# Longformer attention and snake MLP on one core: w_out matmuls placed earlier, index arithmetic moved to batch 0, global columns split

## The chip, the core and the metric

The kernel runs on one core of a Trainium2 chip. The metric is device time in microseconds (us) of one execution. The engines are PE (TensorE: matmuls, with their weight loads listed as PEld), DVE (VectorE), ACT (ScalarE), POOL (GpSimd) and SP (SyncE, which here only issues DMAs). Each engine works through its own list in order.

## The reference, cut to what matters

Attention over 8 batches, 8 heads, 576 tokens, head width 64. A query sees the keys within 32 positions, and 8 global tokens see and are seen by all. The result, as 4608 rows of 512, goes through an MLP:

```python
scores = where(|i - j| <= 32 or i is global or j is global, q @ k.T / 8, -1e9)
x = (softmax(scores) @ v).transpose(0, 2, 1, 3).reshape(4608, 512)
h = x @ w_in                                  # 512 -> 2048
g = h + sin(alpha * h) ** 2 / (alpha + 1e-9)
out = g @ w_out                               # 2048 -> 512
```

## The kernel before, in words

The kernel writes the order of every engine's work by hand: what the code says first is first in the engine's list. It goes batch by batch, and each batch has two stages.

**Attention** of a batch (`attention`, for batch 0 `attention_first`) runs over four head pairs `hp`. A pair has two rounds of `scores` (14 small matmuls into one PSUM tile `ring`, then Exp on ACT, L980, and the mask product on DVE, L981), the sums of the numerators and denominators (`products`, L1009, 28 small matmuls each), a logarithm and an exponential on ACT as the reciprocal (L813, L820), and a product on DVE into `xT` (L1027). There is one `ring` tile, so a round's matmuls start only when the Exp before them has been read out. DVE also takes the sums of the global queries (`GN`, `GD`, L797).

**gemm1** of a batch (`gemm1`) makes `h` in 16 groups `nt` of 128 columns of w_in. A group is 8 matmuls (L1161) into one of three PSUM tiles `zn`, `zr`, `zd` in turn; then Sin on ACT (L1194), a square on ACT or DVE (L1197, L1199), and a multiply and add on DVE into `H` (L1200), which frees the PSUM tile for the group three later. In the last batch `xT` has 64 more columns, the global queries of all batches, made by `global_rows` (L1066, L1068).

**gemm2** (`gemm2`) multiplies `H` with w_out, in blocks of 128 rows: 16 matmuls 128x512 each (L1247) into one of two tiles `zo`, then a copy on ACT to `osb` (L1252) and stores. Even batches have 4 blocks, odd ones 5. It is a Python generator: `fill(n)` takes n of its matmuls and puts them where the code stands. So the w_out matmuls of batch b fill the gaps that PE has in the attention of batch b + 1 and in its gemm1. How many go where is written in tables: `START` one ahead of the first scores, `FIRST[hp]` after the first round of scores of a pair, `SECOND[hp]` after the second, `NEAR` and `MIDST` around the last pair, `PER_GROUP[nt]` after each gemm1 group, `GROUP_LAST[nt]` in the last batch. The copy of a block is put down when the 17th matmul is asked for, ahead of it. What a batch doesn't use up is carried on to the next.

**The tail.** After the last gemm1 come, on PE, all w_out matmuls still waiting, then the 32 matmuls of `gemm2_globals` (L1272), then gemm2 of batch 7 (80 matmuls, the last block in two halves) with a few matmuls of `judge` in between. `put_globals` (L1234) has POOL copy 8 columns of `H`, each to a column whose place is read from a register; it needs the last group's `H`, and gemm2 of batch 7 needs it. `square_x` (DVE) and `square_w` (ACT) feed `judge`, a check of ranges.

`load_columns` computes from the global indices those column places: seven DVE operations on 1x8 numbers (L1213 to L1225), then 8 register loads on POOL. It stands in the attention of batch 5 (batches count from 0), before the last pair's work is done. In batch 0, `load_lying` (L713) has POOL issue four DMAs with the keys and queries of batch 1: two when the scores of batch 0 are done, two when its last products are done. They land where PE transposes them in gemm1 of batch 0 (`turn_lying`, L729).

Of the kernel before, what the change touches and what calls it, by code (L numbers as in the profile page):

```python
# [10 lines left out]
ALU = mybir.AluOpType  # L11
# [238 lines left out]
def kernel(  # L250
# [11 lines left out]
    nc = tc.nc  # L262
    B, H, S, D = q.shape
# [6 lines left out]
    NHP = H // 2  # L270
# [35 lines left out]
    SG = S + NG * B  # L306
# [154 lines left out]
    for half in range(2):  # L461
        for w, src in ((1, k), (0, q)):
            nc.gpsimd.dma_start(
                out=nat[w][D * half : D * half + HK],
# [23 lines left out]
    for t in (gidx8, gp64):  # L488
        nc.vector.memset(t[:].bitcast(DT.int32), 0)
    nc.sync.dma_start(  # L490
        out=g64[:],
# [286 lines left out]
    xTs = {}  # L778
# [160 lines left out]
    def attention(b, beside):  # L939
# [117 lines left out]
        inverse(last)  # L1057
        nc.scalar.preload_act_table(AF.Sin)
        fill(MIDST)
        numerators(last)  # L1060
        beside(NHP)
        after.release()

    def global_rows(bs):

        nc.vector.reciprocal(out=GR[:, :, :, bs], in_=GD[:, :, :, bs])  # L1066
        if bs.stop == B:
            nc.vector.tensor_tensor(  # L1068
                out=xTs[B - 1][:, :, S:SG], in0=GN[:].rearrange("p h j b -> p h (j b)"),
                in1=GR[:].rearrange("p h j b -> p h (j b)"), op=ALU.mult,  # L1070
            )


    spare = [kflat, vflat]
# [68 lines left out]
    def gemm1(b):  # L1143


        while len(waiting) > 1:
            fill(1)
        xT = xTs[b]
        r0 = (b % 2) * S
        more = b == B - 1  # L1150
        W = SG if more else S
        hr = tc.alloc_tile_pool(name="hr", bufs=1, space=PSUM)
        hs = {}

        def chunks(nt, cs, parts=slice(0, 2)):
            if nt not in hs:
                hs[nt] = (zn, None, zd)[nt % 3] or hr.tile([P, 2, 512], DT.float32, name="zr")
            h = hs[nt]
            for c in cs:
                for h_part, lo, hi in halves(h, W)[parts]:  # L1160
                    nc.tensor.matmul(  # L1161
                        out=h_part, lhsT=w_in[:, c, nt * P : (nt + 1) * P], rhs=xT[:, c, lo:hi],
                        start=(c == 0), stop=(c == CT - 1), skip_group_check=True,
                    )

        on_act = (ON_ACT_FIRST, ON_ACT_SECOND, ON_ACT)[min(b, 2)]
        for nt in range(NT):
            if b == 1 and nt in (10, 12):
                for which, t, y in PLACES[nt - 6 : nt - 4]:
                    place(2, which, t, y, nc.vector.tensor_copy)  # L1170
            if b == 0 and 8 <= nt < 14:
                third, late = divmod(nt - 8, 2)
                place_lying(1 - late, third, nc.scalar.copy if late else nc.vector.tensor_copy)
            if b == 0 and nt == 4:
                turn_kq()
            if b == 0 and nt == 10:

                cast_globals_v()
                for part in range(3):
                    place_globals(1, part, nc.gpsimd.tensor_copy)  # L1180
                load_vg(1)
            if nt == 0:

                for n in range(2):
                    chunks(n, range(CT - 1), slice(0, 2 - more))
                for n in range(2 * more):
                    chunks(n, range(CT - 1), slice(1, 2))
            chunks(nt, range(CT - 1, CT) if nt < 2 else range(CT))
            h = columns(hs[nt], W)
            fill((GROUP_LAST if more else PER_GROUP)[nt])  # L1190
            if b == 0 and nt in (7, 9, 11):
                turn_lying((nt - 7) // 2)
            sb = spool.tile([P, SG], DT.bfloat16, name="sb")
            nc.scalar.activation(out=sb[:, 0:W], in_=h, func=AF.Sin, scale=alphaT[:, nt : nt + 1])  # L1194
            s2 = spool.tile([P, SG], DT.bfloat16, name="s2")
            if nt in on_act:
                nc.scalar.activation(out=s2[:, 0:W], in_=sb[:, 0:W], func=AF.Square)  # L1197
            else:
                nc.vector.tensor_tensor(out=s2[:, 0:W], in0=sb[:, 0:W], in1=sb[:, 0:W], op=ALU.mult)  # L1199
            nc.vector.scalar_tensor_tensor(  # L1200
                out=H2[:, nt, r0 : r0 + W], in0=s2[:, 0:W], scalar=recipT[:, nt : nt + 1], in1=h,
                op0=ALU.mult, op1=ALU.add,
            )
        hr.release()


    columns_of = []

    def load_columns():

        ci = normp.tile([1, 4, NG], DT.int32, name="ci")
        cf = normp.tile([1, 4, NG], DT.float32, name="cf")
        nc.vector.tensor_copy(out=ci[:, 0], in_=gi32[:, 0::2])  # L1213
        nc.vector.tensor_scalar(out=ci[:, 1], in0=ci[:, 0], scalar1=1, scalar2=None, op0=ALU.bitwise_and)
        nc.vector.tensor_copy(out=cf[:, 0:2], in_=ci[:, 0:2])
        nc.vector.tensor_scalar(
            out=cf[:, 2], in0=cf[:, 0], scalar1=float(HALF), scalar2=float(QTR), op0=ALU.is_ge, op1=ALU.mult
        )
        nc.vector.scalar_tensor_tensor(
            out=cf[:, 3], in0=cf[:, 0], scalar=0.5, in1=cf[:, 2], op0=ALU.mult, op1=ALU.add  # L1220
        )
        nc.vector.scalar_tensor_tensor(
            out=cf[:, 3], in0=cf[:, 1], scalar=float(QTR) - 0.5, in1=cf[:, 3], op0=ALU.mult, op1=ALU.add
        )
        nc.vector.tensor_scalar(out=gcol[:], in0=cf[:, 3], scalar1=float(S), scalar2=None, op0=ALU.add)  # L1225
        for j in range(NG):
            columns_of.append(nc.gpsimd.value_load(gcol[0:1, j : j + 1], min_val=S, max_val=2 * S - 1))

# [7 lines left out]
    def gemm2(b):  # L1236
        lo, hi = (0, 4) if b % 2 == 0 else (4, 9)
        for blk in range(lo, hi):
            ops = zo[(blk + b // 2) % 2]
            osb = osbp.tile([P, DM], DT.float32, name="osb")  # L1240
            parts = 2 if (b, blk) == (B - 1, hi - 1) else 1
            for part in range(parts):
                cols = slice(part * DM // parts, (part + 1) * DM // parts)
                if part:
                    ops = zd[:, 1]
                for nt in range(NT):
                    nc.tensor.matmul(  # L1247
                        out=ops[:, cols], lhsT=H2[:, nt, blk * P : (blk + 1) * P], rhs=w_out[:, nt, cols],
                        start=(nt == 0), stop=(nt == NT - 1), skip_group_check=True,
                    )  # L1250
                    yield True
                nc.scalar.copy(out=osb[:, cols], in_=ops[:, cols])  # L1252
                store(b, blk, osb, cols)

    def store(b, blk, osb, cols):
# [27 lines left out]
        )  # L1283


    waiting = []

    def fill(n):
        while n and waiting:
            if next(waiting[0], None) is None:  # L1290
                waiting.pop(0)
            else:
                n -= 1

    START = 1
    FIRST, SECOND = (10, 6, 4, 4), (4, 4, 4, 4)

    NEAR, MIDST = 3, 6
    PER_GROUP = (0, 0, 5) + 11 * (1,) + (0, 0)
    GROUP_LAST = (0, 0, 3) + 13 * (1,)  # L1300

    def places_at(b_att, at):
# [5 lines left out]
    def phase_a(b_att, b_moe):  # L1308
        def beside(at):

            if b_moe is None:
                if at == 0:
                    second_half()
                    gather(v, gv)
                if at == NHP - 1:
                    load_lying(0)
                if at == NHP:
                    load_lying(1)
                    cast_v(1)
                    for half in range(2):  # L1320
                        rows = slice(half * D, (half + 1) * D)
                        nc.sync.dma_start(out=MASKT[rows], in_=MASK[rows, half * NT6 : (half + 1) * NT6])
                    load_w_out()
                    load_v(1)
                return
            if at == 2 and b_att == B - 1:
                global_rows(slice(0, B - 1))
            if b_att == 5 and at == 3:
                load_columns()
            if 0 <= at < 2:  # L1330
                square_x(b_moe, at)
            if at == 2 and 1 < b_att and b_att + 2 < B:
                pace(xTs[b_att][0:1, 0, 0:1])
                cast_qk(b_att + 2)
                cast_v(b_att + 2)
            if b_moe == 0 and at == 1:
                turn_qk(2)
            for which, t, y in places_at(b_att, at):
                place(b_att + 1, which, t, y, nc.vector.tensor_copy)

        if b_moe is not None:
            waiting.append(gemm2(b_moe))
        attention(b_att, beside)

    phase_a(0, None)
    for b in range(B):
# [5 lines left out]
        if 0 < b < B - 1:  # L1352
            load_v(b + 1)
            load_vg(b + 1)
        if b == B - 1:
            global_rows(slice(b, B))
        gemm1(b)
        if b + 1 < B:
            if b == 0:
# [54 lines left out]
```

## Time and profile before

| | us |
|---|---|
| median of 3 runs | 361.01 (360.44 to 361.14) |
| the profiled execution, its own time | 360.89 |
| its span, from first to last instruction | 359.1 |
| PE busy in the span | 325.6 |
| ACT busy | 286.4 |
| DVE busy | 274.8 |
| POOL busy | 58.9 |

The profiled execution's own time is 1.8 us above its span, and 0.12 us below the median. A PE that is busy is not a PE at its peak, since ends of matmuls are modelled: in the timeline's rows a matmul's end lies after the start of the next. A delay on PE is therefore best read from starts.

### The profile page before, as it was taken

What the parts mean: (1) busy time and instruction counts of PE and PEld (TensorE: products, weight loads), DVE (VectorE), ACT (ScalarE), POOL (GpSimd) and SP (SyncE); (2) the same over time, 40 slices, a digit from 0 to 9 for tenths busy, and PEclk for the clock granted to TensorE, in tenths of its full rate; (3) what the DMA queues carried; (4) which work ended last, traced back from release to release, by engine and by line L of the source; (5) the groups of instructions that cost most, each with busy time, mean ns of one, the idle gap of its engine ahead of it and who ended that gap; (6) DMA issues with size and microseconds to landing.
All of it is one profiled execution on the core that took longest, in us unless ns stands there. A gap on an engine that the chain in (4) does not pass through costs nothing.

```text
span 359.1 us, 10959 instructions
## 1 busy us (share of the span) xinstructions
PE 325.6 (91%) x4484; PEld 206.8 (58%) x4484; DVE 274.8 (77%) x536; ACT 286.4 (80%) x428; POOL 58.9 (16%) x85
## 2 busy tenths in 40 slices
PE   2668888999899999999999999899999998999992
PEld 1557655556555765577557655576567655664552
DVE  6876866887979787978798788878887876788620
ACT  7779768987889898988998889688988887887510
POOL 7965410051004000400040004000000000004200
PEclk9999989999999999999999999999999999999998
DMA  7999999669988936695759754993251021002132
GB/s 111 114 142 158 160 222 239 143 107 206 189 147 163 171 71 153 126 187 100 133 112 185 146 103 90 197 144 84 63 112 42 2 62 35 29 0 58 51 87 67
DMA packets 87764, 42.27 MB, mean 118 GB/s; under 512 B 72378, under 2 KB 82362, under 8 KB 87322
## 3 DMA queue, kind: packets, MB, share of 16 engines
q0 software_dynamic: 44944, 18.52, 43.1%
q1 hardware_dynamic: 42762, 22.98, 29.1%
q8 instruction: 37, 0.61, 0.7%
q14 instruction: 21, 0.17, 0.2%
HBM read 41.97 MB, written 20.77 MB: 175 GB/s over the span
## 4 chain that ended last, share of the span: by engine, by line
PE 57%; ACT 14%; DVE 13%; DMA 7%; issue 5%; POOL 2%; DVEq 0%; ACTq 0%; POOLq 0%
PE zo L1247 25%; PE zn L1161 9%; DVE H L1200 6%; PE zr L1161 6%; PE zd L1161 5%; ACT sb L1194 5%; PE ring L971 3%; DMA VD<-in_q_dram 3%; DMA H<-in_q_dram 3%; PE zd L1009 2%; DVE s L1199 2%; ACT L947 2%; ACT E L980 2%; ACT s L1197 2%; PE zn L1009 2%
## 5 line engine op out<-in xcount | busy, mean ns | idle before, releaser
L1247 PE MATMUL zo<-w_out,H 128*128 128x512 bf16 (+1 forms) x576 | 148.8, 377 | 0.2 <-DVE E L981 0.2
L1161 PEld LDWEIGHTS <-w_in 128*128 128x128 bf16 x1024 | 99.5, 98 | 49.2 <-issue 16.4
L1247 PEld LDWEIGHTS <-H 128*128 128x128 bf16 x592 | 52.5, 98 | 44.9 <-issue 0.5
L1161 PE MATMUL zn<-xT,w_in 128*128 128x288 bf16 (+1 forms) x384 | 57.0, 287 | 6.9 <-DVE H L1200 3.6
L1194 ACT ACTIVATE sb<-zn,alphaT 128x576 bf16<-128x576 f32 (+1 forms) x48 | 35.7, 743 | 19.5 <-PE zn L1161 19.3
L1161 PE MATMUL zr<-xT,w_in 128*128 128x288 bf16 x320 | 47.8, 288 | 2.1 <-DVE H L1200 2.1
L980 ACT ACTIVATE E<-ring 128x720 bf16<-128x720 f32 x56 | 43.4, 775 | 7.4 <-PE ring L971 6.6
L1200 DVE SCALAR_TENSOR_TENSOR H<-s,recipT,zn 128x576 bf16<-128x576 bf16 (+1 forms) x48 | 39.5, 822 | 11.6 <-ACT s L1197 8.2
L1161 PE MATMUL zd<-xT,w_in 128*128 128x288 bf16 x320 | 47.2, 292 | 0.4 <-DVE H L1200 0.3
L1197 ACT ACTIVATE s<-sb 128x576 bf16<-128x576 bf16 (+1 forms) x58 | 40.0, 689 | 1.8
L981 DVE TENSOR_TENSOR E<-E,MASKT 128x720 bf16<-128x720 bf16 x56 | 29.6, 529 | 14.4 <-ACT E L980 14.1
L1199 DVE TENSOR_TENSOR s<-sb 128x576 bf16<-128x576 bf16 (+1 forms) x70 | 32.0, 458 | 10.5 <-ACT sb L1194 10.5
L1200 DVE SCALAR_TENSOR_TENSOR H<-s,recipT,zr 128x576 bf16<-128x576 bf16 (+1 forms) x40 | 32.9, 822 | 8.8 <-ACT s L1197 6.8
L1200 DVE SCALAR_TENSOR_TENSOR H<-s,recipT,zd 128x576 bf16<-128x576 bf16 (+1 forms) x40 | 32.9, 822 | 6.1 <-ACT s L1197 3.7
L1194 ACT ACTIVATE sb<-zr,alphaT 128x576 bf16<-128x576 f32 (+1 forms) x40 | 29.6, 741 | 8.1 <-PE zr L1161 8.1
L1194 ACT ACTIVATE sb<-zd,alphaT 128x576 bf16<-128x576 f32 (+1 forms) x40 | 29.5, 738 | 4.6 <-PE zd L1161 4.6
L1252 ACT COPY osb<-zo 128x512 f32<-128x512 f32 (+1 forms) x36 | 20.7, 576 | 13.0 <-PE zo L1247 6.7
L820 ACT ACTIVATE R<-L,shift 128x576 f32<-128x576 f32 x32 | 24.9, 778 | 0.5
L347 POOL COPY seen<-xT 1x1 bf16<-1x1 bf16 x4 | 1.7, 428 | 126.6 <-DVE GN L797 126.6
L1234 POOL COPY H<-H 128x16 bf16 x8 | 5.0, 630 | 103.8 <-DVE H L1200 103.4
L1027 DVE TENSOR_TENSOR xT<-zn,R 128x576 bf16<-128x576 f32 x21 | 15.8, 753 | 0.8 <-ACT R L820 0.6
L343 POOL DMA_DIRECT2D vd<-in_v_dram x7 | 16.4, 2337 | 0.1
(185 smaller groups left out, 373.0 us busy)
## 6 DMA issues: line engine op xcount, KB each, us to landing
vd<-in_v_dram POOLq DMA_DIRECT2D x7, 576.0 KB, 14.0
kd<-in_k_dram POOLq DMA_DIRECT2D x6, 576.0 KB, 7.3
qd<-in_q_dram POOLq DMA_DIRECT2D x6, 576.0 KB, 10.2
VX<-vd SPq DMA_DIRECT2D x16, 168.0 KB
w_in<-in_moe_w_in_dram POOLq DMA_DIRECT2D x4, 512.0 KB, 6.7
w_out<-in_moe_w_out_dram POOLq DMA_DIRECT2D x4, 512.0 KB, 19.0
VD<-vd SPq DMA_DIRECT2D x12, 168.0 KB
out_dram<-osb SPq DMA_DIRECT2D x7, 256.0 KB
```

The source lines that it names most:

```text
L343: nc.gpsimd.dma_start(out=cast[b, "vd"][:], in_=v[b].rearrange("h s d -> s h d"))
L820: nc.scalar.activation(out=R[:], in_=L[:], func=AF.Exp, scale=-1.0, bias=shift[:, 0:1])
L980: nc.scalar.activation(out=Eg, in_=zs[:, :, 0 : G3 * WCOL], func=AF.Exp, scale=scale)
L981: nc.vector.tensor_tensor(out=Eg, in0=Eg, in1=MASKT[:, None, G3 * g : G3 * (g + 1), :].rearrange("p o m c -> p o (m c)").to_broadcast([P, ...
L1027: nc.vector.tensor_tensor(out=xT[:, hp, 0:S].rearrange("p (k m c) -> p k m c", k=4, c=KT), in0=tokens(nd(hp, 0)), in1=Rs[hp][:], op=ALU.mult,)
L1161: nc.tensor.matmul(out=h_part, lhsT=w_in[:, c, nt * P : (nt + 1) * P], rhs=xT[:, c, lo:hi], start=(c == 0), stop=(c == CT - 1), skip_group ...
L1194: nc.scalar.activation(out=sb[:, 0:W], in_=h, func=AF.Sin, scale=alphaT[:, nt : nt + 1])
L1197: nc.scalar.activation(out=s2[:, 0:W], in_=sb[:, 0:W], func=AF.Square)
L1199: nc.vector.tensor_tensor(out=s2[:, 0:W], in0=sb[:, 0:W], in1=sb[:, 0:W], op=ALU.mult)
L1200: nc.vector.scalar_tensor_tensor(out=H2[:, nt, r0 : r0 + W], in0=s2[:, 0:W], scalar=recipT[:, nt : nt + 1], in1=h, op0=ALU.mult, op1=ALU.add,)
L1247: nc.tensor.matmul(out=ops[:, cols], lhsT=H2[:, nt, blk * P : (blk + 1) * P], rhs=w_out[:, nt, cols], start=(nt == 0), stop=(nt == NT - 1) ...
L1252: nc.scalar.copy(out=osb[:, cols], in_=ops[:, cols])
```

## The change

Five edits, each a place in an engine's list:

1. `FIRST[0]` goes from 10 to 12: two more w_out matmuls ahead of the second scores of the first pair, in batches 1 to 7.
2. `AFTER_COPY`: in gemm1, two groups after one in which a block's copy was put down, two more w_out matmuls.
3. `PER_GROUP` puts one more at group 14.
4. The seven DVE operations on the column places become `find_columns` and move into the attention of batch 0, at the end of the third pair; the register loads stay.
5. In the last batch the reciprocal of the global sums and the products of three of the four pairs' global columns go ahead of the last numerators; the fourth pair's product follows them. Before, one reciprocal and one product came after all.

```diff
         fill(MIDST)
+        if b == B - 1:
+            global_rows(slice(b, B))
+            global_columns(slice(0, last))
         numerators(last)
+        if b == B - 1:
+            global_columns(slice(last, NHP))
         beside(NHP)
...
     def global_rows(bs):
         nc.vector.reciprocal(out=GR[:, :, :, bs], in_=GD[:, :, :, bs])
-        if bs.stop == B:
-            nc.vector.tensor_tensor(
-                out=xTs[B - 1][:, :, S:SG], in0=GN[:].rearrange("p h j b -> p h (j b)"),
-                in1=GR[:].rearrange("p h j b -> p h (j b)"), op=ALU.mult,
-            )
+
+    def global_columns(hps):
+        nc.vector.tensor_tensor(
+            out=xTs[B - 1][:, hps, S:SG], in0=GN[:, hps].rearrange("p h j b -> p h (j b)"),
+            in1=GR[:, hps].rearrange("p h j b -> p h (j b)"), op=ALU.mult,
+        )
...
         for nt in range(NT):
+            at_group[0] = (b, nt)
...
             fill((GROUP_LAST if more else PER_GROUP)[nt])
+            if nt and copied[0] == (b, nt - 2):
+                fill(AFTER_COPY)
...
-    def load_columns():
+    def find_columns():
...
+    def load_columns():
         for j in range(NG):
...
                 nc.scalar.copy(out=osb[:, cols], in_=ops[:, cols])
+                copied[0] = at_group[0]
...
-    FIRST, SECOND = (10, 6, 4, 4), (4, 4, 4, 4)
+    FIRST, SECOND = (12, 6, 4, 4), (4, 4, 4, 4)
+    AFTER_COPY = 2
...
-    PER_GROUP = (0, 0, 5) + 11 * (1,) + (0, 0)
+    PER_GROUP = (0, 0, 5) + 12 * (1,) + (0,)
...
                 if at == 0:
                     second_half()
                     gather(v, gv)
+                if at == 2:
+                    find_columns()
...
-        if b == B - 1:
-            global_rows(slice(b, B))
         gemm1(b)
```

What this makes of the lists, at three places. Names are tiles; `[waits X]` says on which engine's semaphore an instruction waits.

**PE, the tail.** Before, from the last of the waiting w_out matmuls (L1247, 37 of them after the last gemm1 group) through the 32 of `gemm2_globals` (L1272) to the first of batch 7's gemm2:

```order
L1247 LDWEIGHTS H_97
L1247 MATMUL zo_124<-w_out,H_97 128x512
L1272 LDWEIGHTS H_97
L1272 MATMUL zd<-w_out,H_97 64x256 [waits DVE_49]
...
L1247 LDWEIGHTS H_97 [waits Pool_49]
L1247 MATMUL zo_125<-w_out,H_97 128x512 [waits Activation_49]
```

With the change, from the last gemm1 group (L1168) on; what stands in the rows left out first is five more w_out matmuls (L1261), then `gemm2_globals` (L1287):

```order
L1168 LDWEIGHTS w_in
L1168 MATMUL zn<-xT,w_in 128x352
L1261 LDWEIGHTS H_97
L1261 MATMUL zo_124<-w_out,H_97 128x512
...
L1287 LDWEIGHTS H_97
L1287 MATMUL zd<-w_out,H_97 64x256 [waits DVE_49]
...
L1261 LDWEIGHTS H_97 [waits Pool_49]
L1261 MATMUL zo_125<-w_out,H_97 128x512 [waits Activation_49]
```

Between the last group and `gemm2_globals` 6 w_out matmuls are left of 37: 31 stand earlier, 14 of them in the attention of batches 1 to 7 (two each), and in gemm1 of batches 1 to 7 there are -2, +3, +3, +3, +3, +5 and +2. The weight load that waits for POOL stands where it stood.

**DVE, the end of the attention of batch 7.** Before, with the last numerators' product (`xT<-zd`) and the global columns (`xT<-GN,GR`):

```order
L797 TENSOR_REDUCE GD<-zr 128x2x4
L1027 TENSOR_TENSOR xT<-zd,R 128x576
L797 TENSOR_REDUCE GN<-zd 128x2x4
L1066 RECIPROCAL GR<-GD 128x32
L1068 TENSOR_TENSOR xT<-GN,GR 128x4x64
```

With the change:

```order
L797 TENSOR_REDUCE GD<-zr 128x2x4
L1071 RECIPROCAL GR<-GD 128x32
L1075 TENSOR_TENSOR xT<-GN,GR 128x3x64
L1027 TENSOR_TENSOR xT<-zd,R 128x576
L797 TENSOR_REDUCE GN<-zd 128x2x4
L1075 TENSOR_TENSOR xT<-GN,GR 128x64
```

Only the last 64 columns' product is left behind the last numerators.

**DVE, batch 0**, between the second pair's product into `xT` (L897) and the three mask products (L847) of the fourth pair:

```order
 L897 TENSOR_TENSOR xT<-zn,R 128x576
+L1224 COPY ci<-girow 1x8
+L1225 TENSOR_SCALAR ci<-ci 1x8
+L1226 CAST cf<-ci 1x16
+L1227 TENSOR_SCALAR cf<-cf 1x8
+L1230 SCALAR_TENSOR_TENSOR cf<-cf 1x8
+L1233 SCALAR_TENSOR_TENSOR cf<-cf 1x8
+L1236 TENSOR_SCALAR gcol<-cf 1x8
 L847 TENSOR_TENSOR E<-E,MASK 128x480 x3
```

The seven rows are those that stood in the attention of batch 5, ahead of its last two products into `xT`.

More of the change, by code (lines that the diff above doesn't have):

```diff
@@ L1204, in gemm1 @@
         hr.release()
+        at_group[0] = None
     columns_of = []
-    def load_columns():
+    def find_columns():
         ci = normp.tile([1, 4, NG], DT.int32, name="ci")
@@ L1283, in gemm2_globals @@
         )
-    waiting = []
+    waiting, copied, at_group = [], [None], [None]
     def fill(n):
```

## The prediction

> **What bounds the kernel now.** I read the page first, then the chain of waits, then the timeline at the places that the change touches.
>
> ```profile
> span 359.1 us, 10959 instructions
> PE 325.6 (91%) x4484; PEld 206.8 (58%) x4484; DVE 274.8 (77%) x536; ACT 286.4 (80%) x428; POOL 58.9 (16%) x85
> PE 57%; ACT 14%; DVE 13%; DMA 7%; issue 5%; POOL 2%; DVEq 0%; ACTq 0%; POOLq 0%
> ```
>
> PE is busy for 91% of the span and holds 57% of the chain: from batch 1 on it is the bound, broken by short waits. The change adds no PE work, so it can win only waits of PE. The second thing to read is the end, in the chain of waits.
>
> ```profile
> 324.73 7.99 PE zo L1247 x37
> 332.72 1.87 PE zd L1272 x32
> 334.58 7.01 PE zo L1247 x32
> ...
> 352.87 0.37 ACT osb L1252
> ```
>
> After the last gemm1 group, at T = 324.73, PE has no gap to 352.85: 37 w_out matmuls at 7.99/37 = 0.216 us each, the 32 of the globals, then batch 7's gemm2 from 334.58 on, 9.85 after T. A w_out matmul taken from these 37 seems to be worth 0.216 us. But behind them another chain is hidden, seen in the timeline:
>
> ```profile
> 326.53 0.88 DVE L1200 SCALAR_TENSOR_TENSOR H<-s,recipT,zn 128x640 bf16<-128x640 bf16 x1
> 327.48 5.46 POOL L1234 COPY H<-H 128x16 bf16 x8 [103.39 <-DVE H L1200]
> ```
>
> POOL's eight copies start when the last H is made and end at 332.94, T + 8.21. Batch 7's gemm2 waits for them. PE comes to it 1.6 us later now, so the wait costs nothing. This is the point on which the forecast turns.
>
> **The change, part by part.** T moves by the PE work that is put ahead of it, less the waits that go.
>
> *Work ahead of T.* 31 matmuls (37 - 6) x 0.216 = +6.70.
>
> *Second scores (edit 1).* In a batch's first pair PE waits for ACT:
>
> ```profile
> 98.35 2.33 PE L1247 MATMUL zo<-w_out,H 128*128 128x512 bf16 x10
> 100.01 0.77 ACT L980 ACTIVATE E<-ring 128x720 bf16<-128x720 f32 x1
> 100.83 0.35 PE L971 MATMUL ring<-QX,KD 64*64 64x120 bf16 x14
> ...
> 287.82 0.35 PE L971 MATMUL ring<-QX,KX 64*64 64x120 bf16 x14
> ```
>
> The ten matmuls take 2.16 from 98.35, to 100.51; elsewhere scores start 0.09 after a w_out matmul is through, so 0.22 of the start at 100.83 is the wait for the Exp that ends at 100.78. The same 0.22 stands in batches 2, 3, 5, 6 and 7 (the last row is batch 7's), 0.15 in batch 4 and none in batch 1: 5 x 0.22 + 0.15 = -1.25. Two matmuls (0.43) cover it, so each batch's attention gets about 0.2 longer.
>
> *Copies and group 14 (edits 2 and 3).* A block's copy on ACT holds up a Sin, and so a PSUM tile:
>
> ```profile
> 131.46 0.57 ACT L1252 COPY osb<-zo 128x512 f32<-128x512 f32 x1
> 134.13 1.14 PE L1161 MATMUL zn<-xT,w_in 128*128 128x288 bf16 x8 [0.48 <-DVE H L1200]
> ...
> 312.48 0.38 PE L1247 MATMUL zo<-w_out,H 128*128 128x512 bf16 x1
> 313.06 1.25 PE L1161 MATMUL zr<-xT,w_in 128*128 128x288 bf16 x8 [0.21 <-DVE H L1200]
> ```
>
> The first copy, at 131.46, is followed by the wait at 134.13. At 313.06 a group starts 0.58 after a matmul of 0.216: 0.37 of waiting. From the first (0.64) to this there are nine such waits, at the third group after a copy or at group 15: 0.64 in batch 2, 0.40 in 3, 0.43 and 0.26 in 4, 0.39 and 0.22 in 5, 0.43 and 0.25 in 6, 0.37 in 7, together 3.39. Two matmuls stand now where 0.37 to 0.43 was waited, one where 0.22 to 0.26 was: -3.39. What is late next is PE itself. In batch 1, where two fewer stand, DVE's placing copies set the pace at the end, and I count no wait won or lost.
>
> *Column places (edit 4).* In batch 5 seven small operations stand between other work of DVE:
>
> ```profile
> 224.03 0.15 DVE L1213 COPY ci<-girow 1x8 int32<-1x8 int32 x1
> 225.37 0.46 DVE L369 COPY KD<-kt 64x1152 bf16<-64x1152 bf16 x1
> 227.74 0.53 PE L1161 MATMUL zn<-xT,w_in 128*128 128x288 bf16 x3 [1.17 <-DVE GN L797]
> ```
>
> The seven hold DVE 225.37 - 224.03 = 1.34 us, and gemm1 then waits 1.17 for the product and sum behind them. Without them that is 1.34 earlier, the numerators on PE are next, and 1.13 goes. POOL's register loads stay, and POOL stands idle for 103.39 between them and the copies that use them (row above).
>
> In batch 0 the same 1.34 lands here (rows of the timeline, of the chain, and of the DMA issues with KB and us to landing):
>
> ```profile
> 29.35 1.22 DVE L847 TENSOR_TENSOR E<-E,MASK 128x480 bf16<-128x480 bf16 x3
> 30.20 0.79 PE L878 MATMUL zr<-E,OB 128*128 128x88 bf16 x14
> 31.38 0.63 ACT L813 ACTIVATE L<-zr 128x576 f32<-128x576 f32 x1
> 32.08 0.58 POOL VD L713
> 32.66 10.86 DMA VD<-in_q_dram
> 43.02 0.21 PE L729 MATMUL zo<-identb,KD 48*64 48x48 bf16 x1
> 43.56 0.21 PE L729 MATMUL zo<-identb,VD 48*64 48x48 bf16 x1 [0.34 <-DMA VD<-in_q_dram]
> KD<-in_k_dram POOLq DMA_DIRECT2D x1, 288.0 KB, 9.7
> VD<-in_q_dram POOLq DMA_DIRECT2D x1, 288.0 KB, 10.9
> ```
>
> The masks would end at 31.91 instead of 30.57. PE, ready for these products at 30.20, is through 1.2 later, and so is POOL's issue of the last two loads at 32.08; behind them on POOL's queue stand batch 1's values and w_out. ACT's logarithm of these sums, at 31.38, can start at 32.27, 0.9 later, and with it gemm1. PE's transposes, reached at 43.02, wait until 43.56 for the load that lands at 43.52. Between nothing and the whole 1.2 I take +0.45, near the row of that wait: PE comes 0.9 late, and 0.5 of waiting covers half of it. The landing itself should hardly move: the first load was issued 2.5 ahead of the last and needed 9.7, the last 10.9, so they drain one behind another, and the last has to queue anyway.
>
> *Global columns (edit 5).* The chain of waits shows what gemm1 of batch 7 waits for:
>
> ```profile
> 302.10 0.76 DVE xT L1027
> 302.86 0.13 DVE GN L797
> 302.99 0.27 DVE GR L1066
> 303.29 0.43 DVE xT L1068
> ...
> 303.77 0.61 PE zn L1161 x3
> ```
>
> The six half groups ahead are through by 302.63. With the reciprocal and three pairs' product ahead of 302.10, in DVE's wait for the numerators, PE goes on; the last quarter's product is due about 303.25, ahead of the matmul that needs it. 303.77 - 302.63 = -1.14.
>
> So T moves by 6.70 - 1.25 - 3.39 - 1.13 - 1.14 + 0.45 = **+0.24**. The waits removed are just paid for by the work moved ahead.
>
> *The tail.* After T there are 6 x 0.216 + 1.87 = 3.2 us of PE work, and then the wait for POOL. POOL's copies end at T + 8.21 as before: H, the squares beside them and ACT's work stand in the same order. With weight load and issue PE goes on at about T + 8.4, where it was T + 9.85: -1.45. PE now stands idle for 5.2 us. What that does to its clock is in the views by window:
>
> ```profile
> 46.41:49.82 3.41, 1.85 (x72) 1.44 (x72) 2.28 (x4) 1.80 (x4) 0.22 (x1) 1.00 1.23 223
> 49.82:53.23 3.41, 3.22 (x70) 2.02 (x71) 1.62 (x3) 2.81 (x5) 0.00 (x0) 0.50 1.21 229
> 56.65:60.06 3.41, 2.45 (x27) 1.44 (x27) 2.67 (x5) 3.36 (x6) 0.00 (x0) 1.00 1.22 250
> 353.59:357.00 3.41, 0.00 (x0) 0.00 (x0) 0.00 (x0) 0.00 (x0) 0.00 (x0) 1.00 0.16 46
> 357.00:360.41 3.41, 0.00 (x0) 0.00 (x0) 0.00 (x0) 0.00 (x0) 0.00 (x0) 0.50 0.05 12
> ```
>
> (The first two numbers after the length are busy time of PE and its loads, PEclk is third from the end.) After a stretch of 3.41 us with 1.56 of it idle the granted clock was 0.50 for the next 3.41; after one with 0.96 idle it stayed at 1.00; after an empty one, at the end, it fell. A gap of 5.2 holds at least 2.6 of idle time in one stretch, wherever their borders fall. The next stretch then runs at half clock, filled with w_out matmuls on the path that sets the end: 3.41/2 = +1.7 (0.9 if the gap reaches far into it, 2.6 if two are touched).
>
> The Trainium skill (TensorE: Matmul & The Clock Gate, section Part 1: The HAM clock gate) says that the clock halves after an idle window of about 3.4 us and returns after a busy one, in windows that run free of the kernel. The trace agrees with its 3.41 us, and shows a fall after a window that was only part idle. The rule speaks against this change, and by it the sum has the same +1.7.
>
> The wait of 0.3 for DVE inside judge shrinks too, since DVE gets more time: -0.1. The sum is 0.24 - 1.45 + 1.7 - 0.1 = +0.4. The profiled execution stands at 360.89, the median of the runs 0.12 above; I put it on the median: **361.4 us**.
>
> **The rivals.**
>
> *The clock holds* (faster). All as above, but PE goes on at full clock after the gap: 361.0 - 1.3 = 359.7. For it: the windows' thresholds are known from three rows only. Against it: 2.6 idle is well over 1.56. Chance 0.16.
>
> *The loads of batch 0 come late* (slower). The whole 1.2 passes through the last load, because POOL issues it 1.2 later and its 10.86 stays. Then 0.75 more than counted: 362.2. It decides if the landing moves by more than 0.35 past 43.52. For it: the chain goes through this load. Against: the queue drains in order. Chance 0.22.
>
> *POOL is quicker* (faster). One row shows how uneven its copies are:
>
> ```profile
> L1234 POOL COPY H<-H x8: 256/466/1452, 327.5 to 332.7; 128x16 bf16 x8
> ```
>
> The first, beside DVE's square of 1.48 us, took 1.45; the last three, with DVE still, 0.26 each. If DVE's work slid away from them, eight at 0.26 with 0.05 between would end by T + 5.2, the gap be 2.2 and the clock stay: about 361.0 + 0.2 - 4.5 = 356.7. The order of DVE's work is unchanged, so chance 0.04. The Trainium skill (SBUF — State Buffer, section SBUF: two separate sides) says that DVE and GpSimd hold a shared port pair by an exclusive lock for a whole instruction; the spread from 0.26 to 1.45 agrees.
>
> *The moved matmuls don't meet the waits*: each block's copy now falls at another group, and new waits of 0.2 arise. This widens the forecast's own spread to ±0.8, and no more, as batches 2 to 7 had the copies at different groups and yet the same waits.
>
> **How the numbers follow.** Forecast 0.58, centre +0.4: within 0.2% (0.72 us, about what a measurement of this kernel can tell from no change) 0.39, slower 0.16, faster 0.03. Clock holds 0.16: faster 0.14, within 0.02. Late loads 0.22: slower 0.21, within 0.01. Quick POOL 0.04: faster. Together faster 0.21, within 0.42, slower 0.37. Forecast's own range 360.6 to 362.2; the range takes in the late loads with a longer half clock at one end and the clock that holds at the other: 359.7 to 362.6.
>
> **What would show it.** In the changed profile: PE without work for about 5 us ahead of batch 7's gemm2, released by POOL H; 0.50 in PEclk after it; T at 325.0; second scores right behind their twelve matmuls; no 1.17 at gemm1 of batch 5 and none at the global columns; the transposes of batch 0 about 0.45 later. It is wrong if the gap is short, if PEclk stays at 1.00, or if T moves by more than 1 us.

## The result and the profile after

| | before | after |
|---|---|---|
| median, us | 360.8 (22 runs, 359.7 to 361.7) | 362.1 (22 runs, 360.8 to 363.8) |
| ratio to before | | 1.0041, 95% interval 1.0029 to 1.0052 |
| the profiled execution's own time, us | 360.89 | 361.52 |
| its span, us | 359.1 | 359.7 |

The change makes the kernel slower by 0.41%, 1.5 us (1.0 to 1.9). The forecast was 361.4 us, +0.4, in a range of 359.7 to 362.6; the median lies inside it, but "slower" (chance 0.37) came and not the likelier "within 0.2%" (0.42). One execution of before at 818 us is left out of its spread (the median without it is 360.7).

The page of the changed kernel: its span, the busy time of the engines, the clock granted to PE in 40 slices of 9 us, and the engines' shares of the chain.

```profile
span 359.7 us, 10897 instructions
PE 319.2 (89%) x4427; PEld 206.9 (58%) x4484; DVE 274.0 (76%) x537; ACT 287.3 (80%) x428; POOL 59.2 (16%) x85
PEclk9999989999999999999999999999999999999898
PE 46%; issue 31%; ACT 8%; DVE 5%; DMA 3%; POOL 3%; POOLq 1%; another core or an unknown queue 1%; DVEq 0%; ACTq 0%
```

57 matmul records are missing from this trace (4427 where the program has 4484), so PE's lower busy time is no saving; I read starts. The 8 in the third slice from the end of PEclk is new: a stretch at half clock in the tail. The chain's shares can't be set against those of before, since it loses its thread ("issue" 31%) for 100 us. Its end is whole:

```profile
328.17 1.43 POOL H L1248
...
331.59 1.06 POOL H L1248
...
333.56 0.27 POOL H L1248
333.83 0.05 issue
333.88 1.46 PE zo L1261 x3
...
353.53 0.37 ACT osb L1266
```

Before, PE alone carried the end of the chain from T on. Now the eight copies of POOL carry it from 328.17 to 333.83, and PE has nothing to do until 333.88. The timeline shows the hole from PE's side:

```profile
326.75 1.94 PE L1287 MATMUL zd<-w_out,H 128*64 128x256 bf16 x32
328.15 5.67 POOL L1248 COPY H<-H 128x16 bf16 x8 [102.61 <-DVE H L1210]
333.88 1.46 PE L1261 MATMUL zo<-w_out,H 128*128 128x512 bf16 x3 [5.19 <-POOL H L1248]
```

And the windows around it show the clock (third number from the end):

```profile
329.99:333.41 3.42, 0.00 (x0) 0.00 (x0) 3.29 (x7) 3.22 (x4) 3.12 (x6) 1.00 0.13 40
333.41:336.83 3.42, 2.74 (x6) 1.05 (x8) 3.31 (x8) 1.08 (x1) 1.34 (x3) 0.50 0.18 38
336.83:340.25 3.42, 3.42 (x17) 1.57 (x16) 2.14 (x2) 0.59 (x1) 0.00 (x0) 1.00 0.00 0
```

PE does nothing for a whole window, and the next runs at 0.50. Of its 3.42 us, 2.95 lie behind 333.88 and are paid for. All of this stands as forecast, to 0.3 us.

The places where waits were to go. First the second scores of a first pair (batch 7), then gemm1 of batch 5:

```profile
286.85 2.76 PE L1261 MATMUL zo<-w_out,H 128*128 128x512 bf16 x12
289.55 0.35 PE L971 MATMUL ring<-QX,KX 64*64 64x120 bf16 x14
```
```profile
227.52 0.50 PE L1009 MATMUL zd<-E,VX 56*64 56x88 bf16 x28
227.96 0.90 PE L1168 MATMUL zn<-xT,w_in 128*128 128x288 bf16 x6
```

Twelve matmuls take 12 x 0.216 = 2.59, to 289.44, and the scores follow at 289.55: the wait of 0.22 is gone. gemm1 of batch 5 starts 0.44 behind the last numerators with no releaser named, so the wait of 1.17 is gone too. A wait that the kernel before does not have stands in batch 6, at the group after the first five w_out matmuls of gemm1:

```profile
269.99 1.14 PE L1168 MATMUL zn<-xT,w_in 128*128 128x288 bf16 x8 [0.29 <-DVE H L1210]
```

Last, batch 0, where the column indices went. Rows of the timeline, and one of the chain (the load in flight):

```profile
29.45 0.15 DVE L1224 COPY ci<-girow 1x8 int32<-1x8 int32 x1
30.67 1.03 DVE L847 TENSOR_TENSOR E<-E,MASK 128x480 bf16<-128x480 bf16 x3
31.12 0.99 PE L878 MATMUL zr<-E,OB 128*128 128x88 bf16 x14 [0.59 <-DVE E L847]
33.17 0.59 POOL L713 DMA_DIRECT2D VD<-in_k_dram  x1 [1.62 <-PE zd L878]
```
```profile
33.75 10.81 DMA VD<-in_q_dram
```
```profile
44.61 0.21 PE L729 MATMUL zo<-identb,VD 48*64 48x48 bf16 x1 [0.70 <-DMA VD<-in_q_dram]
```

Seven small operations of DVE (29.45 is the first, the last starts at 30.59) now stand ahead of the masks at 30.67. PE waits for the masks, POOL issues the last two loads 1.09 later than before (33.17 for 32.08), and the last lands 1.04 later (44.56 for 43.52). In the prediction this chain is the rival "the loads of batch 0 come late", not the forecast.

### The profile page after: what moved, and what is told of

Same layout as the page of the kernel before. It is cut to its first block, busy times and chain, and to the rows that moved or that the text cites. A ratio compares the mean times of both kernels' runs of the same rounds, so it can differ in the third digit from the quotient of the medians.

```text
span 359.7 us, 10897 instructions
## 1 busy us (share of the span) xinstructions
PE 319.2 (89%) x4427; PEld 206.9 (58%) x4484; DVE 274.0 (76%) x537; ACT 287.3 (80%) x428; POOL 59.2 (16%) x85
## 4 chain that ended last, share of the span: by engine, by line
PE 46%; issue 31%; ACT 8%; DVE 5%; DMA 3%; POOL 3%; POOLq 1%; another core or an unknown queue 1%; DVEq 0%; ACTq 0%
PE zo L1261 21%; PE zn L1168 6%; PE zr L1168 5%; PE zd L1168 5%; DMA VD<-in_q_dram 3%; PE ring L971 3%; DVE H L1210 2%; ACT KD L627 2%; ACT sb L1204 2%; PE zd L1009 2%; POOL H L1248 1%; PE zn L1009 1%; POOLq L1241 1%; ACT s L1207 1%
## 5 line engine op out<-in xcount | busy, mean ns | idle before, releaser
L1261 PE MATMUL zo<-w_out,H 128*128 128x512 bf16 (+1 forms) x519 | 136.6, 379 | 11.5 <-issue 5.8
L1168 PEld LDWEIGHTS <-w_in 128*128 128x128 bf16 x1024 | 99.7, 98 | 44.2 <-issue 9.7
L1261 PEld LDWEIGHTS <-H 128*128 128x128 bf16 x592 | 52.9, 98 | 50.1 <-POOL H L1248 5.5
L1168 PE MATMUL zn<-xT,w_in 128*128 128x288 bf16 (+1 forms) x384 | 57.0, 287 | 3.3 <-DVE H L1210 2.8
L1168 PE MATMUL zr<-xT,w_in 128*128 128x288 bf16 x320 | 48.4, 290 | 1.4 <-DVE H L1210 1.4
L1168 PE MATMUL zd<-xT,w_in 128*128 128x288 bf16 x320 | 47.2, 292 | 0.5
```

The source lines that it names most:

```text
L1168: nc.tensor.matmul(out=h_part, lhsT=w_in[:, c, nt * P : (nt + 1) * P], rhs=xT[:, c, lo:hi], start=(c == 0), stop=(c == CT - 1), skip_group ...
L1261: nc.tensor.matmul(out=ops[:, cols], lhsT=H2[:, nt, blk * P : (blk + 1) * P], rhs=w_out[:, nt, cols], start=(nt == 0), stop=(nt == NT - 1) ...
```

## The experiments

Eleven kernels were run, each in five rounds, against the kernel before on the same chip. They ran in three groups (e1 to e4, e5 to e8, e9 to e11), and the median of before was 360.1, 360.8 and 361.0 in them; so kernels of different groups are compared by their ratios.

| run | what it is | median, us | ratio to before (95%) |
|---|---|---|---|
| e1_fills | before + edits 1 to 3 | 363.49 | 1.0104 (1.0075 to 1.0133) |
| e2_no_fills | before + edits 4 and 5 | 358.29 | 0.996 (0.9942 to 0.9977) |
| e11_globals | before + edit 5 | 359.7 | 0.9963 (0.9943 to 0.9983) |
| e4_cols_back | after without edit 4 | 362.14 | 1.0063 (1.0041 to 1.0085) |
| e3_warm | after, PE kept busy in the gap | 359.53 | 0.9989 (0.997 to 1.0008) |
| e5_pool_alone | after, DVE held back beside POOL | 358.03 | 0.992 (0.9888 to 0.9951) |
| e6_cols_end | after, column indices a pair later | 364.43 | 1.0104 (1.0079 to 1.0128) |
| e7_best | e6 + e5's tail + 12 matmuls left in the tail | 358.88 | 0.9947 (0.9927 to 0.9967) |
| e8_before_pool | before + e5's tail | 360.19 | 0.999 (0.9977 to 1.0004) |
| e9_tail12 | after + e5's tail + 12 matmuls left in the tail | 356.99 | 0.9879 (0.9858 to 0.99) |
| e10_tail12_cols5 | e9 without edit 4 | 357.3 | 0.989 (0.987 to 0.9911) |

The same starts of PE in one profiled execution of each (us; T here is the start of the last gemm1 group's last matmul, 0.31 ahead of the T of the prediction; "into batch 5" is from the last gemm1 matmul of batch 4 to the first of batch 5; the last column is from the first to the last w_out matmul of batch 7, all starts):

| run | end of gemm1, batch 0 | into batch 5 | gemm1 of batch 7 | T | gemm2 of batch 7 starts | it lasts |
|---|---|---|---|---|---|---|
| before | 57.79 | 18.65 | 22.53 | 324.42 | 334.52 | 18.04 |
| after | 58.90 | 17.64 | 21.47 | 325.09 | 333.88 | 19.34 |
| e1 | 57.50 | 18.87 | 22.59 | 326.86 | 335.64 | 19.93 |
| e2 | 57.40 | 17.43 | 21.40 | 321.13 | 331.23 | 18.04 |
| e11 | 57.92 | 18.64 | 21.40 | 322.95 | 333.05 | 18.05 |
| e4 | 57.09 | 18.86 | 21.46 | 324.36 | 333.15 | 19.87 |
| e3 | 57.23 | 17.64 | 21.46 | 323.96 | 332.75 | 17.91 |
| e5 | 58.88 | 17.64 | 21.47 | 325.78 | 331.37 | 19.59 |
| e6 | 61.56 | 17.64 | 21.46 | 327.64 | 336.42 | 19.39 |
| e7 | 61.24 | 17.63 | 21.38 | 327.44 | 332.70 | 17.90 |
| e8 | 57.47 | 18.64 | 22.52 | 323.76 | 333.86 | 17.91 |
| e9 | 58.85 | 17.64 | 21.39 | 325.57 | 330.83 | 17.91 |
| e10 | 57.67 | 18.85 | 21.38 | 325.50 | 330.76 | 17.90 |

### The moved matmuls alone

```diff
-    FIRST, SECOND = (10, 6, 4, 4), (4, 4, 4, 4)
+    FIRST, SECOND = (12, 6, 4, 4), (4, 4, 4, 4)
+    AFTER_COPY = 2
...
-    PER_GROUP = (0, 0, 5) + 11 * (1,) + (0, 0)
+    PER_GROUP = (0, 0, 5) + 12 * (1,) + (0,)
...
+            if nt and copied[0] == (b, nt - 2):
+                fill(AFTER_COPY)
```

> The kernel before with edits 1 to 3 alone (the w_out matmuls moved ahead; column places stay in batch 5, global columns in one piece). Theory (the matmuls taken from the tail uncover POOL's copies, and the gap halves PE's clock): T moves by 6.70 - 1.25 - 3.39 = +2.1 and nothing comes back in the tail: batch 7's gemm2 starts about 0.7 later than before, half clock adds 1.3 to 2, so 362.8 to 363.5, 0.6 to 0.8% slower than before. Rival (the moved matmuls are free, and the loss is edit 4's in batch 0): at or below the time before, 359.5 to 361.

Measured: 1.04% slower (0.75 to 1.33), at the upper side of what was expected or above. From the end of gemm1 in batch 0 to T the profile has 269.36 where before has 266.63: +2.73 for a sum of 6.70 - 1.25 - 3.39 = +2.06. By batch, from the first to the last gemm1 matmul and from there to the next batch's first, batches 2 to 7 take 2.17 longer (2.05 in the sum), the attentions 1.35 of it (1.34 in the sum). The other 0.55 is in batch 1, for which the sum has nothing. gemm2 of batch 7 starts 8.78 after T for 10.10, and lasts 1.89 longer. Windows of this kernel:

```profile
332.90:336.30 3.40, 0.66 (x2) 0.28 (x3) 3.33 (x7) 3.16 (x2) 2.44 (x5) 0.51 0.01 2
336.40:339.70 3.30, 3.30 (x9) 1.21 (x8) 3.13 (x7) 0.00 (x0) 1.00 (x1) 0.50 0.19 40
```

Here two stretches ran at half clock, one of them mostly inside the gap, so 4.1 us at half clock were paid for instead of 2.95. What follows: the moved matmuls are the loss. They hide waits worth less than they cost ahead of T, and the tail gives back 1.3 us and takes it again through the clock.

### The other two edits, and one of them alone

e2 is the changed kernel with edits 1 to 3 undone, so 37 matmuls stand in the tail; e11 is e2 with `find_columns` back in batch 5.

```diff
-    FIRST, SECOND = (12, 6, 4, 4), (4, 4, 4, 4)
-    AFTER_COPY = 2
+    FIRST, SECOND = (10, 6, 4, 4), (4, 4, 4, 4)
+    AFTER_COPY = 0
...
-    PER_GROUP = (0, 0, 5) + 12 * (1,) + (0,)
+    PER_GROUP = (0, 0, 5) + 11 * (1,) + (0, 0)
```

> The changed kernel with edits 1 to 3 undone, so edits 4 and 5 alone: 37 w_out matmuls are left for the tail again. Theory: batch 0 loses 0.5 to 1.1, batch 5 gains 1.1, the global columns gain 1.1, the tail has no gap and PEclk stays at 1.00 there: 359.4 to 360.2, 0.2 to 0.4% faster than before. Rival (edit 4 costs more than it gives): 361 or more.

> The kernel before with the global columns ahead of the last numerators as its only change; the column indices stay in batch 5 and no w_out matmul is moved. As the prediction has this edit, gemm1 of the last batch starts 1.14 us earlier and 37 w_out matmuls cover GpSimd's copies: ratio 0.997. If the two edits without the fills (ratio 0.996 together) owe their gain to the column indices, this is within 0.1% of the kernel before; if they owe it to the global columns alone, it is 0.996 or less.

Measured: 0.4% faster (0.23 to 0.58) and 0.37% faster (0.17 to 0.57), both as forecast. The tail of e2:

```profile
321.28 8.15 PE L1261 MATMUL zo<-w_out,H 128*128 128x512 bf16 x37
324.19 5.47 POOL L1248 COPY H<-H 128x16 bf16 x8 [101.40 <-DVE H L1210]
329.36 1.94 PE L1287 MATMUL zd<-w_out,H 128*64 128x256 bf16 x32
331.23 5.14 PE L1261 MATMUL zo<-w_out,H 128*128 128x512 bf16 x23
```

POOL is through at 329.66, 1.57 ahead of the matmul that needs it, and PE has no gap. Edit 5 takes gemm1 of batch 7 from 22.53 to 21.40, -1.13 for a forecast of -1.14. Edit 4 takes the way into batch 5 from 18.65 to 17.43 (e2), or with the fills from 18.86 to 17.64: -1.22 for a forecast of -1.13.

### The column indices taken back

```diff
-                if at == 2:
-                    find_columns()
...
+                find_columns()
                 load_columns()
```

> The changed kernel with edit 4 undone: the seven operations on the column places stand in batch 5 again. Theory (edit 4 loses 1.1 in batch 0 by the late loads and wins 1.1 in batch 5): gemm1 of batch 1 about 1.1 earlier than in the changed kernel, gemm1 of batch 5 waits 1.2 again, the total as the changed kernel, 361.8 to 362.4. Rival (batch 0 takes it at no cost): 363.2.

Measured: 1.0063 beside the changed kernel's 1.0041, with intervals that overlap. The pairs e2 and e11 (0.996, 0.9963) and e9 and e10 (0.9879, 0.989) stand the same way round, and overlap as well. So edit 4 gains between nothing and 0.2%; no single pair resolves it. The profiles show where its 1.22 goes.

In batch 0 the ends of gemm1 in the table can't be set side by side as they stand, because executions already differ ahead of edit 4's place. The first of POOL's four loads waits for an Exp on ACT that edit 4 does not touch, and it is issued anywhere from 29.77 to 30.84 (first row after, second e2):

```profile
30.28 0.65 POOL L713 DMA_DIRECT2D KD<-in_k_dram  x1 [5.98 <-ACT E L846]
29.88 0.65 POOL L713 DMA_DIRECT2D KD<-in_k_dram  x1 [4.69 <-ACT E L846]
```

Counted from this issue, gemm1 of batch 0 ends 28.62, 27.52, 27.27, 28.04 and 28.17 later with edit 4 (after, e2, e3, e5, e9; mean 27.92), and 27.61, 27.73, 27.35, 26.84, 27.13 and 27.02 later without (before, e1, e11, e4, e8, e10; mean 27.28): 0.64 given back. Part of the rest of the spread goes with the clock: after, e9, before and e1, the longest of their lists, each have a stretch of 3.41 us at half clock near 50 us, and the other seven have none. Like beside like, edit 4 costs 0.73 with that stretch and 0.52 without it.

In batch 6 another part goes. From its first to its last matmul, gemm1 of batch 6 takes 20.63 in after and e9 and 20.62 in e3 and e5, which have edit 4, and 20.27 in e1, e4 and e10, which have the same fills without it; 20.19 in e2 against 19.82 to 19.84 in before, e8 and e11. So 0.36 is given back in every profile that has edit 4, at the wait of 0.29 shown above (e2 has the same wait at its 266.75). Why a wait moves there is not shown. Together -1.22 + 0.64 + 0.36 = -0.2 us, too little for the intervals to tell from nothing.

### PE kept busy in the gap

Twenty-two matmuls of ones whose result nobody reads stand behind the globals' product.

```diff
     gemm2_globals()
+    for _ in range(22):
+        nc.tensor.matmul(
+            out=zn[:, 0, :], lhsT=ones[:], rhs=ones[:][:, None, :].to_broadcast([P, 4, P]),
+            start=True, stop=True, skip_group_check=True,
+        )
     judge_sums()
```

> The changed kernel with 22 matmuls of ones into a free PSUM tile (4.75 us of PE work whose result nobody reads) in the gap ahead of batch 7's gemm2. Theory (half clock after the gap costs 1.3 to 2): PEclk stays at 1.00, batch 7's gemm2 starts as in the changed kernel and takes 18.3 instead of 19.6: 360.1 to 360.8, within 0.2% of before. Rival (the clock is a label, the loss lies ahead of the tail): 362.1 as the changed kernel.

Measured: 0.9989 (0.997 to 1.0008), where the changed kernel has 1.0041 (1.0029 to 1.0052). The tail of e3:

```profile
327.02 5.67 POOL L1248 COPY H<-H 128x16 bf16 x8 [102.60 <-DVE H L1210]
327.50 4.92 PE L1389 MATMUL zn<-ones 128*128 128x512 bf16 x22
332.75 1.47 PE L1261 MATMUL zo<-w_out,H 128*128 128x512 bf16 x6 [0.34 <-POOL H L1248]
```

POOL and the start of gemm2 are where they were (T + 8.79 in both), and nothing useful was added. Only the clock differs: gemm2 of batch 7 lasts 17.91 instead of 19.34. So the half clock is shown to cost 0.52% of the time by the two ratios (1.9 us; with both intervals 1.1 to 2.7) and 1.43 us in the two profiles. The mean granted clock of every execution is on record too: 0.987 over the 22 of the changed kernel, 0.993 over the 12 of e3, a difference of about 2.1 us of full-speed clock. The gap itself is not what is paid for: gemm2 of batch 7 still starts 1.31 closer to T than before.

### POOL without VectorE beside it

DVE reads one element that POOL's last copy writes, ahead of the squares of `judge`, and so waits until the copies are done. `judge`'s sums follow one block later.

```diff
     put_globals()
-    square_x(B - 1, 0)
-    square_x(B - 1, 1)
     square_w(0)
-    fill(NT)
-    square_w(1)
-    fill(4 * NT)
+    fill(5 * NT)
     gemm2_globals()
-    judge_sums()
+    placed = normp.tile([1, 1], DT.bfloat16, name="placed")
+    nc.vector.tensor_copy(out=placed[:], in_=H2[0:1, 0, S : S + 1])
+    square_x(B - 1, 0)
+    square_x(B - 1, 1)
     waiting.append(gemm2(B - 1))
-    for c in (2, 3):
+    for c in (1, 2, 3):
...
+    judge_sums()
     judge()
```

> The changed kernel, with DVE held back in the tail: behind the globals' copy DVE reads one number that POOL writes, so its squares, sums and range tests start when POOL's eight copies are through; judge stands one block of w_out matmuls later. Theory (POOL's copies take 0.26 each when DVE is quiet, and PE waits for them): the copies take 2.5 instead of 5.67, the gap shrinks from 5.4 to 2.2, batch 7's gemm2 starts 3.2 earlier; the clock stays, or falls for one stretch if the gap lies in one window: 0.5 to 0.9% faster than before. Rival (POOL's copies are slow by themselves): same gap, 0.4 to 0.6% slower than before.

Measured: 0.992 (0.9888 to 0.9951), 0.8% faster than before. The tail, then two windows (the first holds the gap):

```profile
328.83 2.48 POOL L1248 COPY H<-H 128x16 bf16 x8 [102.61 <-DVE H L1210]
331.37 4.88 PE L1261 MATMUL zo<-w_out,H 128*128 128x512 bf16 x14 [2.00 <-POOL H L1248]
```
```profile
328.60:332.00 3.40, 1.40 (x18) 0.81 (x14) 1.24 (x4) 3.19 (x5) 2.06 (x8) 1.00 0.26 77
332.00:335.40 3.40, 3.40 (x9) 1.21 (x8) 3.30 (x5) 1.39 (x1) 1.02 (x1) 0.50 0.17 39
```

The eight copies take 2.48 instead of 5.67. They are the same copies, and ACT is as busy beside them (3.19 of 3.40 us); what is gone from beside them is DVE's squares. The gap shrinks from 5.2 to 2.0, and still a stretch at half clock follows it in this execution. The six executions spread from 355.9 to 359.7, with mean clocks from 0.989 to 0.997, the fastest at 0.997; so not all had the same stretches at half clock. The Trainium skill (SBUF — State Buffer, section SBUF: two separate sides) has DVE and GpSimd exclude each other from a shared port pair for whole instructions: this run agrees, and puts a number on it, 3.2 us over eight copies of 0.26.

The same tail on the kernel before is the control, since there 37 matmuls cover POOL anyway.

> The kernel before with the same tail (DVE held back until POOL is through, judge one block later), a control. Theory (before, 37 w_out matmuls cover POOL's copies, so quicker copies are worth nothing): within 0.2% of before. Rival (the tail is faster by itself, or DVE's later work holds judge up): 0.3% or more to either side.

Measured: 0.999 (0.9977 to 1.0004). A quicker POOL alone is worth 0.2% at most; it pays where PE waits for it.

### The column indices a pair later: a theory that fell

```diff
-                if at == 2:
-                    find_columns()
...
                 if at == NHP:
+                    find_columns()
                     load_lying(1)
```

> The changed kernel with find_columns behind the last pair of batch 0's attention instead of the third. Theory (in the third pair its 1.34 us hold up the last products and POOL's issue of two loads): masks, products and issue in batch 0 as in the kernel before, 0.3 to 1 faster than the changed kernel, so 0.1 to 0.35% slower than before. Rival (its place is hidden in batch 0): as the changed kernel, 0.4% slower than before.

Measured: 1.0104 (1.0079 to 1.0128), slower than with edit 4 as it is. The idea was that behind the last pair's work they delay neither masks nor loads. The loads did go out earlier (31.77 for 33.17, of which 0.41 is an earlier start of the batch). But:

```profile
32.92 2.25 POOL L343 DMA_DIRECT2D vd<-in_v_dram  x1
33.23 2.15 DVE L1224 COPY ci<-girow 1x8 int32<-1x8 int32 x1
...
38.24 1.06 PE L1168 MATMUL zn<-xT,w_in 128*128 128x288 bf16 x7 [3.12 <-DVE H L1210]
```
```profile
35.69:39.10 3.41, 0.86 (x8) 0.68 (x7) 3.15 (x9) 0.96 (x2) 1.74 (x3) 1.00 0.89 147
39.10:42.51 3.41, 3.41 (x20) 2.22 (x18) 2.44 (x5) 1.42 (x2) 0.75 (x1) 0.50 1.63 169
```

The copy of eight integers, 0.15 us elsewhere, took 2.15 beside POOL's issue of a large load (2.17 in e7, at the same place). PE's wait in gemm1 at 38.24 became 3.12, and behind this hole a stretch ran at half clock. The changed kernel at the same group:

```profile
37.14 1.14 PE L1168 MATMUL zn<-xT,w_in 128*128 128x288 bf16 x8 [1.06 <-DVE H L1210]
```

The hole is 2.06 longer in e6, about the 2.0 that the copy took longer. gemm1 of batch 0 ended at 61.56 for 58.90. That POOL's issue is what held the copy is argued from the rows that lie side by side, not shown by a run that takes the issue away.

### Two versions with both causes treated

e7 has the column indices as in e6, e5's tail, and

```diff
-    GROUP_LAST = (0, 0, 3) + 13 * (1,)
+    GROUP_LAST = (0, 0, 3) + 6 * (0, 1) + (0,)
```

so that of the seventeen w_out matmuls that stand between the last batch's groups six go to the tail, 12 in all.

> A version to beat both: the changed kernel with DVE held back as in the run with POOL alone, find_columns behind the last pair of batch 0, and in gemm1 of batch 7 a w_out matmul at every second group only, which leaves 12 for the tail instead of 6. Theory: the gap is 2.2 - 6 x 0.216 = 0.9 or less, the clock stays at 1.00, 0.9 to 1.2% faster than before. Rival (gemm1 of batch 7 gets no shorter without those matmuls): 0.6 to 0.9%.

Measured: 0.9947 (0.9927 to 0.9967), less than expected, since batch 0 pays for the place of the column indices again (its gemm1 ends at 61.24). The tail is as meant: gemm2 of batch 7 lasts 17.90. So e9 puts the column indices back to where the change has them, and e10 back to batch 5.

> The changed kernel, with the column indices where the change puts them in batch 0, with the tail of the kernel in which VectorE is held back until GpSimd's eight copies are done, and with six of the eighteen w_out matmuls that the last batch's groups take left to the tail, so that TensorE has 12 matmuls and the global rows' product to do there. Theory (the changed kernel loses in the gap and in the half clock behind it, and nowhere else): the gap closes to under 1 us, the clock stays at 1.0 behind it, and the time is that of the run that held VectorE back alone (ratio 0.992) less the half clock that was left there (0.3 to 0.5%): ratio 0.987 to 0.990. Rival (what the run with the column indices behind the last pair gave, 0.9947, is all that this tail can bring, and its slow batch 0 cost nothing): ratio 0.994 to 0.996. Second rival (the half clock in batch 0 and not that in the tail sets what differs between executions): ratio as with VectorE held back alone, 0.992.

> The run beside it with the column indices taken back to batch 5, as before the change. If they are worth the 1.13 us less 0.45 us of the prediction, this is 0.2% slower than the run beside it; if their eight operations cost batch 0 what they save in batch 5, the two are within 0.1%; if batch 0's start is held up by them by over 1 us, as the one profile of the changed kernel shows, this is up to 0.2% faster.

Measured: 0.9879 (0.9858 to 0.99) and 0.989 (0.987 to 0.9911). The tail of e9, and the windows around POOL's copies:

```profile
325.72 2.75 PE L1261 MATMUL zo<-w_out,H 128*128 128x512 bf16 x12
328.29 2.49 POOL L1248 COPY H<-H 128x16 bf16 x8 [102.19 <-DVE H L1210]
328.40 1.94 PE L1287 MATMUL zd<-w_out,H 128*64 128x256 bf16 x32
330.83 3.41 PE L1261 MATMUL zo<-w_out,H 128*128 128x512 bf16 x14 [0.49 <-POOL H L1248]
```
```profile
326.98:330.40 3.42, 3.36 (x39) 2.15 (x37) 1.14 (x2) 2.13 (x3) 1.75 (x7) 1.00 0.09 25
330.40:333.81 3.41, 2.92 (x13) 1.39 (x15) 2.96 (x5) 3.41 (x3) 1.30 (x3) 1.00 0.16 52
```

The gap is 0.5, the clock stays at 1.00 there, and the kernel is 1.2% faster than before (1.0 to 1.4), the best of all that were run. The moved matmuls that cost 1.04% alone are not a loss in themselves: with a tail that goes on at once, the kernel that has them stands 0.8% below the one that has only the other two edits (0.9879 beside 0.996). It also has the quicker POOL, but by e8 that alone is worth 0.2% at most where the tail covers it.

## Why the prediction came out as it did

The mechanism of the tail was right, and the size of the whole too small: +0.4 us was forecast, +1.5 (1.0 to 1.9) measured. By its own steps:

- *Work ahead of T less waits* (+2.06 for edits 1 to 3): +2.73, +2.46 and +2.24 by the pairs before and e1, e2 and after, e11 and e4, from the end of gemm1 in batch 0 to T. In batches 2 to 7 it is 2.17 for 2.05, the same within 0.02 in all three pairs, so the waits went as counted. The excess is in batch 1, where the step "I count no wait won or lost" goes wrong: the two matmuls that its gemm1 loses were counted as 0.43 won, but it took +0.26, -0.04 and -0.10 in the three pairs. Its attention took +0.29, +0.33 and +0.17 for 0.43. Together that is +0.3 on the mean, with a spread as large as itself.
- *Column places leave batch 5* (-1.13): -1.22. *Global columns* (-1.14): -1.13. Both right. That a wait comes up in batch 6 instead (+0.36) was not foreseen.
- *Column places in batch 0* (+0.45): +0.64 on the mean, by a reason that failed in part, "The landing itself should hardly move: the first load was issued 2.5 ahead of the last". In the changed kernel's profile the first pair of loads was issued as before (30.28 for 30.18), the last pair 1.09 later, and the last landed 1.04 later, 10.81 after its issue as it had been 10.86. Counted from the first load's issue, it lands at 13.27 to 14.28 in the five profiles with edit 4 and at 12.41 to 13.34 in the six without, 0.78 later on the mean. The rival "late loads" had a chance of 0.22 and its sign was met in the profile, but its whole 1.2 was not paid.
- *T*: +0.67 in the profile for +0.24.
- *The tail*: gemm2 of batch 7 starts 1.31 closer to T, for 1.45. The difference is in "POOL's copies end at T + 8.21 as before": they took 5.67 for 5.46.
- *The half clock* (+1.7, 0.9 to 2.6): 1.9 by the ratios of after and e3, 1.43 between their profiles, and one or two stretches by execution (e1 and e4 show 6.8 us of it). Mechanism and size right. *Clock holds* is refuted.
- *judge* (-0.1): 17.91 for 18.04, -0.13.

With the measured terms: 0.64 (batch 0) + 0.3 (batch 1) + 2.17 - 1.22 + 0.36 (batch 6) - 1.13 = +1.1 for T, then -1.31 + 1.9 - 0.13, together +1.6, inside the measured 1.0 to 1.9. Several small terms, each of 0.1 to 0.4 and all on the slow side, make the difference between forecast and result; the largest two, batch 6 and batch 1, were put at nothing. The two profiled executions differ by only 0.63 in their own time, since that of the changed kernel is one of its shorter ones (361.52 for a median of 362.1) and that of before one of its longer (360.89 for 360.7).

The rival that POOL could be quicker was worked out at 356.7, a ratio of 0.988, with a gap of 2.2 and a clock that stays. It did not come by itself. Brought about on purpose (e5), the gap was 2.0, close to what was worked out, but the clock fell in the profile, and the ratio was 0.992; with the gap closed as well (e9) it was 0.9879.

What stays open: why batch 0 meets a half-clock stretch near 50 us in some executions and not in others; why gemm1 of batch 6 gets a wait when the seven operations leave batch 5; and edit 4's own worth, which lies within the intervals.

## What to carry to other kernels

Matmuls that wait at the end of a kernel may be hiding another engine's chain; before they are moved forward, work out how long that chain takes and leave as many behind as cover it. Where PE falls idle on the path, add the half clock behind the hole to the price, which here was larger than what the move had gained in the tail. And look first at what makes the covered chain slow: here VectorE beside GpSimd doubled it. With that removed the same change turned from 0.4% slower into 0.8% faster, and with twelve matmuls left behind instead of six into 1.2%.

## What the runs showed of the hardware that was not expected

- A gap of 2.0 us, 1.40 us of work in a window of 3.40, was enough for a half-clock stretch behind it (e5). The Trainium skill (TensorE: Matmul & The Clock Gate, section Part 1: The HAM clock gate) speaks of an idle window of 3.4 us; here a part-idle one did it, so a gap shorter than a window isn't safe. Over the 3.41 us stretches of all thirteen profiles from 27 us on, the clock never fell behind one with 1.36 us idle or less, and always behind one with 1.55 or more; between 1.37 and 1.48 it fell behind some (e6 at 49.32, e9 at 47.61) and stayed behind others (e5 at 41.84, e6 at 329.21). PE's busy time is modelled, so this is no sharper rule.
- After a 5.2 us gap the clock stayed at half for one stretch of 3.41 us in some kernels' profiles (after, e6) and for 6.83 in others (e1, e4).
- GpSimd's copy of 128x16 took 0.26 us alone and up to 1.45 beside VectorE's products of two bf16 operands.
- A VectorE copy of eight integers took 2.15 us beside a GpSimd DMA issue of 2.25, and 0.15 elsewhere.
